# Feed-forward kernel whose second weight matrix is stored with reversed columns and streamed from the last column to the first

## The chip, the cores and the metric

The kernel runs on one core of one Trainium2 chip. The metric is device time in microseconds (us) for one execution of the whole program. A single execution was also taken by the hardware profiler; its rows are what the argument below is made from.

## The reference

The program computes three stages over 4608 tokens (8 batches of 576) of width 512. What matters here is the second, a dense feed-forward layer with a softplus between two products:

```
def _moe_ref(x, w_in, w_out):            # x 4608x512, w_in 512x2048, w_out 2048x512
    h = x @ w_in
    g = np.maximum(h, 0.0) + np.log1p(np.exp(-np.abs(h)))
    return (g @ w_out).astype(np.float32)

def reference(...):
    attn_out = _attn_ref(q, k, v)         # attention over keys pooled by 8; 8 heads of 64
    x = attn_out.transpose(0, 2, 1, 3).reshape(B * S, H * D)
    x = _moe_ref(x, w_in, w_out)          # the layer above
    return _moe2_ref(x, w_skip, w_gate, w1, w2)   # 8 experts, one per token, 512->1024->512, or skipped
```

## The kernel before, in words

The tokens are worked through in nine groups of 512 (`G`); `NG` is 9. For each group the attention of the next group runs in small pieces between the matmuls of the current one. The hidden width of 2048 is cut into 16 blocks `c` of 128.

`p1(g, c)` makes one block of the hidden layer: 12 matmuls accumulate `h`, 128 hidden rows by 512 tokens. ScalarE and VectorE then form the softplus and split it into a high part `gh` and a low part `gl`. `p2(g, c, gh, gl)` multiplies that block with rows `128c` to `128c+127` of the second matrix. It fills four PSUM tiles `y0` to `y3`, one for each 128 tokens of the group, and runs three matmuls into each: high by high, high by low, and low by high. In these matmuls the stationary operand (`lhsT`, loaded into the array ahead of the product) is a piece of `gh` or `gl`, 128 by 128. The moving operand (`rhs`, streamed through the array one column after the other) is the high or the low part of the second matrix, 128 by 512.

The loop calls `p1` for block `c` and, two blocks later, `p2` of that same block, so the softplus of a block has two blocks of time. `p2` is thus called 9 x 16 = 144 times with 12 matmuls each, 1728 matmuls in all (lines 641, 642 and 643, 576 each). The order on every engine is the order in which the program is written here.

The weights stay in SBUF for all nine groups. `_layout` packs them on the host with `words`: for each block `c`, 512 numbers of `w_in` and then 512 of `w_out`, in 8-byte form. `load_weights` fetches them once (tile `raw`), rebuilds 32-bit numbers from the two 4-byte halves, and writes their high and low parts into the tiles `wt`. There, in each row of 1024 numbers, columns 0 to 511 belong to `w_in` and columns 512 to 1023 to `w_out`. The two halves in `raw` are 4-byte numbers at a step of 8 bytes (`raw[:, :, 0]` and `raw[:, :, 1]`), so lines 455 and 458 read and write on ScalarE at that step and line 464 reads at it, while line 624 and line 628 work on plain consecutive 4-byte numbers.

After the last group the expert layer follows (`superblock`); its own matrices are `w1` and `w2`, and the lines of its products are 783 and 802 to 804.

Of the kernel before, what the change touches and what calls it, by code (L numbers as in the profile page):

```python
# [20 lines left out]
P = 128  # L21
# [13 lines left out]
def tile_kernel(ctx, tc, qT, kT, vT, wbits, w9, w1, w2, out):  # L35
# [364 lines left out]
    with ExitStack() as ph:  # L400
# [39 lines left out]
        def load_weights():  # L440


            bits = wbits.bitcast(I32)
            for c in range(16):
                if c % 2 == 0:
                    wt.append(wtile(f"wt{c // 2}", 2, 2, 1024, dtype=F32R))
                for j in range(2):
                    wh, wl = (wt[c // 2][:, c % 2, i, j * 512:(j + 1) * 512] for i in range(2))
                    raw = scratch.tile([P, 512, 2], I32, tag="raw", name="raw")
                    nc.sync.dma_start(out=raw.rearrange("p a b -> p (a b)"),  # L450
                                      in_=bits[c * P:(c + 1) * P, j * 1024:(j + 1) * 1024])
                    lo, hi = raw[:, :, 0], raw[:, :, 1]


                    nc.scalar.activation(out=hi.bitcast(F32), in_=hi.bitcast(F32), func=AF.Copy,
                                         scale=2.0 ** -112)

                    nc.scalar.activation(out=lo, in_=lo.bitcast(U32), func=AF.Copy, scale=7.49 * 2.0 ** -32)
                    yield
                    nc.vector.scalar_tensor_tensor(out=lo, in0=hi, scalar=3, in1=lo,  # L460
                                                   op0=ALU.logical_shift_left, op1=ALU.bitwise_or)
                    nc.vector.scalar_tensor_tensor(out=lo, in0=hi, scalar=-0x80000000, in1=lo,
                                                   op0=ALU.bitwise_and, op1=ALU.bitwise_or)
                    nc.scalar.activation(out=wh, in_=lo.bitcast(F32), func=AF.Copy)  # L464
                    yield
                    nc.vector.tensor_tensor(out=wl, in0=lo.bitcast(F32), in1=wh.bitcast(F32),
                                            op=ALU.subtract)
                    yield
# [164 lines left out]
        def p2(g, c, gh, gl):  # L633
            if c == 0:
                yps[g] = [ps_y.tile([P, D], F32, tag=f"y{t}", name=f"y{t}") for t in range(T)]
            w = wt[c // 2][:, c % 2]
            wh, wl = w[:, 0, 512:], w[:, 1, 512:]
            for t in range(T):
                th, tl = gh[:, t * P:(t + 1) * P], gl[:, t * P:(t + 1) * P]
                y = yps[g][t]  # L640
                nc.tensor.matmul(y, lhsT=th, rhs=wh, start=c == 0, stop=False)  # L641
                nc.tensor.matmul(y, lhsT=th, rhs=wl, start=False, stop=False)  # L642
                nc.tensor.matmul(y, lhsT=tl, rhs=wh, start=False, stop=c == 15)  # L643

        wl = load_weights()
# [45 lines left out]
        for g in range(NG):  # L691
            if g + 1 < NG:
                feed.start(units_of(g + 1), 6)
            for c in range(16):
                while loaded[0] < 6 * c + 3:
                    weights(1)
                pend.append((g, c, *p1(g, c)))
                weights(3)
                feed.tick()
                if len(pend) > 2:  # L700
                    item = pend.pop(0)
                    p2(*item)
                    if item[1] == 15:
                        ends.append(finish(item[0], yps[item[0]], lambda: ps_a, "pa"))
                if g == NG - 1:
                    last_group(c)
                weights(3)
                feed.tick()
                if loaded[0] == 96 and "cm9" not in ws:
                    scratch_cm.__exit__(None, None, None)  # L710
                    ws["cm9"] = ctx.enter_context(tc.tile_pool(name="cm9", bufs=1, side="right"))
                    ws["junk"] = ws["cm9"].tile([P, D], BF16, name="junk")
                    fill = ws["cm9"].tile([P, NCOL], I32, tag="fill", name="fill")
                    nc.gpsimd.memset(fill, int(BIG))
                    nc.sync.dma_start(out=tab.rearrange("(p c) b -> p (c b)", p=P), in_=fill)
            while g + 1 < NG and (feed.units or jobs or ends):
                feed.tick()
# [7 lines left out]
        hs = wtile("hs", 2, 8, SB, dtype=F32R)  # L725
        hh, hl = hs[:, 0], hs[:, 1]
        p2(*pend.pop(0))
        turn(0, ps_a, "pa")
        p2(*pend.pop(0))
        t = xp.tile([P, 4 * G], F32, tag="xl", name="xg1")  # L730
        xg[1] = [t[:, j * XW:(j + 1) * XW] for j in range(2)]
# [111 lines left out]
def _layout(q, k, v, moe_w_in, moe_w_out, moe2_w_skip, moe2_w_gate, moe2_w1, moe2_w2):  # L843
    import numpy as np
    B, H, S, Dh = q.shape

    def heads(a):
        return np.ascontiguousarray(a.reshape(B, H // 2, 2, S, Dh).transpose(0, 1, 2, 4, 3)).reshape(
            B * H // 2, 2 * Dh, S)

    def words(a, b):

        n = a.shape[1] // P
        return np.ascontiguousarray(np.concatenate([
            a.reshape(a.shape[0] // P, P, n, P).transpose(2, 1, 0, 3).reshape(n, P, -1),
            b.reshape(n, P, -1)], axis=2)).view(np.int64).reshape(n * P, -1)

    E, DM, F = moe2_w1.shape
    return {
        "qT": heads(q),  # L860
        "kT": heads(k),
        "vT": heads(v),
        "wbits": words(moe_w_in, moe_w_out),
        "w9": np.ascontiguousarray(np.concatenate([moe2_w_gate.T, moe2_w_skip[None, :]], axis=0)),
        "w1": np.ascontiguousarray(moe2_w1.reshape(E, DM // P, P, F).transpose(0, 2, 1, 3)).reshape(
            E * P, DM // P * F),
        "w2": np.ascontiguousarray(moe2_w2.reshape(E, F // P, P, DM).transpose(0, 2, 1, 3)).reshape(
            E * P, F // P * DM),
    }
# [18 lines left out]
```

## Time and profile before

| | |
|---|---|
| median of 3 runs | 1423.46 us (1421.79 to 1427.55) |
| the profiled execution's own time | 1429.72 us |
| its span, first to last instruction | 1428.0 us |
| TensorE matmuls (PE) busy | 1383.2 us, 97% of the span |
| TensorE weight loads (PEld) busy | 1151.9 us, 81% (beside the matmuls) |
| VectorE (DVE) busy | 844.4 us, 59% |
| ScalarE (ACT) busy | 643.2 us, 45% |
| GpSimd (POOL) busy | 313.7 us, 22% |
| mean granted TensorE clock | 0.994 of full speed |

Matmuls are pipelined: a matmul's busy time runs from its start until its result has left the array, and the next one starts before that. The pace of a stream of matmuls is therefore read from the distance between their starts, not from the busy time of one.

### The profile page before, as it was taken

The page shows a single profiled execution, that of the slowest core. Times are in us where ns is not written, and L with a number is a line of the kernel's source. Part 1 is how long each engine was busy: PE and PEld are TensorE (multiplying, and loading weights), DVE is VectorE, ACT ScalarE, POOL GpSimd, SP SyncE. Part 2 cuts the span into 40 slices and gives each one's busy share as a digit, 9 for nine tenths or more (in the row PEclk, how much of TensorE's full clock was granted, in tenths as well). Part 3 has the DMA queues.
Part 4 walks back from the last instruction along what each step waited for, and adds up shares of the span by engine and source line. Part 5 has one row for each costly group of instructions (what it writes and reads, how often), then busy time and mean ns, then how long its engine had stood idle before and what let it go on. Part 6 is the DMA issues. An engine that isn't in the chain of part 4 may idle for free. (4 is left out here: it accounts for less than half of the span.)

```text
span 1428.0 us, 21431 instructions
## 1 busy us (share of the span) xinstructions
PE 1383.2 (97%) x7434; PEld 1151.9 (81%) x7434; DVE 844.4 (59%) x2053; ACT 643.2 (45%) x1204; POOL 313.7 (22%) x365
## 2 busy tenths in 40 slices
PE   4999999999999999999999999999999999999996
PEld 3666877787878878778778778889998988999896
DVE  7888884784883973964954935654453422224254
ACT  5888655554554555555555455551111111113142
POOL 2010021021121121121030120143333433324232
PEclk9999999999999999999999999999999999999998
DMA  6545331131130230320310200502212111114051
GB/s 207 161 155 173 96 108 40 55 108 32 54 115 24 62 108 25 91 84 19 107 46 15 82 23 23 192 16 75 63 50 75 46 46 46 58 34 162 25 228 67
DMA packets 57691, 114.19 MB, mean 80 GB/s; under 512 B 17205, under 2 KB 23477, under 8 KB 56544
## 3 DMA queue, kind: packets, MB, share of 16 engines
q1 hardware_dynamic: 40032, 76.07, 17.3%
q0 software_dynamic: 17536, 36.60, 7.6%
q8 instruction: 62, 1.02, 0.3%
q14 instruction: 61, 0.50, 0.1%
HBM read 166.14 MB, written 29.67 MB: 137 GB/s over the span
## 5 line engine op out<-in xcount | busy, mean ns | idle before, releaser
L620 PE MATMUL h<-xh,wt 128*128 128x512 f32 x1152 | 389.3, 398 | 1.6 <-ACT wt L464 0.8
L620 PEld LDWEIGHTS h<-xh,wt 128*128 128x128 f32 x1152 | 217.1, 189 | 59.5 <-issue 10.4
L118 DVE CUSTOM_DVE_ANT_0 junk<-rows,w9b 128x512 bf16<-128x512 f32 x324 | 234.3, 723 | 9.3 <-ACT rows L112 3.7
L641 PE MATMUL y<-wt,gh 128*128 128x512 f32 x576 | 230.3, 400 | 2.1 <-ACT gh L628 2.1
L783 PE MATMUL h<-xt,w1h 128*128 128x256 f32 x1280 | 226.4, 281 | 3.2 <-ACT w1h L384 1.1
L620 PE MATMUL h<-xl,wt 128*128 128x512 f32 x576 | 226.3, 393 | 0.0
L643 PE MATMUL y<-wt,gl 128*128 128x512 f32 x576 | 224.6, 390 | 0.0
L642 PE MATMUL y<-wt,gh 128*128 128x512 f32 x576 | 224.6, 390 | 0.0
L783 PEld LDWEIGHTS h<-xt,w1h 128*128 128x128 f32 x1280 | 196.1, 188 | 6.0 <-issue 2.2
L626 DVE SCALAR_TENSOR_TENSOR a<-h,a 128x512 f32<-128x512 f32 x144 | 98.9, 687 | 169.6 <-ACT a L625 168.8
L787 ACT ACTIVATE hs<-h 128x512 fp32r<-128x512 f32 x80 | 47.4, 598 | 327.3 <-PE h L783 218.2
L623 ACT ACTIVATE a<-h 128x512 f32<-128x512 f32 x144 | 86.0, 598 | 226.3 <-PE h L620 195.8
L783 PE MATMUL h<-xt,w1l 128*128 128x256 f32 x640 | 179.4, 280 | 0.7 <-DVEq L833 0.7
L533 POOL TENSOR_TENSOR q<-q,st 64x144 f32<-64x144 f32 (+7 forms) x60 | 62.6, 1052 | 520.3 <-ACT xh L571 95.4
L628 ACT ACTIVATE gh<-a 128x512 fp32r<-128x512 f32 x144 | 90.8, 631 | 120.5 <-DVE a L626 119.3
L788 DVE SCALAR_TENSOR_TENSOR hs<-h,hs 128x512 fp32r<-128x512 f32 x80 | 54.7, 691 | 138.8 <-ACT hs L787 106.8
L641 PEld LDWEIGHTS y<-wt,gh 128*128 128x128 f32 x576 | 108.2, 188 | 28.2 <-ACT gh L628 2.9
L620 PEld LDWEIGHTS h<-xl,wt 128*128 128x128 f32 x576 | 108.7, 189 | 23.2 <-issue 2.8
L643 PEld LDWEIGHTS y<-wt,gl 128*128 128x128 f32 x576 | 108.1, 188 | 23.3 <-DVE gl L630 0.4
L642 PEld LDWEIGHTS y<-wt,gh 128*128 128x128 f32 x576 | 108.3, 188 | 20.4
L630 DVE TENSOR_TENSOR gl<-a,gh 128x512 fp32r<-128x512 f32 x144 | 99.3, 689 | 41.4 <-ACT gh L628 39.0
L783 PEld LDWEIGHTS h<-xt,w1l 128*128 128x128 f32 x640 | 122.2, 191 | 0.9 <-DVEq L833 0.9
(181 smaller groups left out, 1991.8 us busy)
## 6 DMA issues: line engine op xcount, KB each, us to landing
w9b<-w SPq DMA_DIRECT2D x81, 256.0 KB
raw<-wbits SPq DMA_DIRECT2D x32, 512.0 KB
x2d<-rows SPq DMA_DIRECT2D x36, 260.0 KB
kv<-kT SPq DMA_DIRECT2D x28, 288.0 KB
kv<-vT SPq DMA_DIRECT2D x28, 288.0 KB
q<-qT SPq DMA_DIRECT2D x8, 224.0 KB
q<-qT SPq DMA_DIRECT2D x8, 192.0 KB
q<-qT SPq DMA_DIRECT2D x8, 160.0 KB
```

The source lines that it names most:

```text
L118: nc.vector.tensor_tensor_reduce(out=ws["junk"], in0=rows[t][:, :D], in1=w9b[e], scale=1.0, scalar=0.0, op0=ALU.mult, op1=ALU.add, accum_o ...
L533: nc.gpsimd.tensor_tensor(out=ep_, in0=ep_, op=ALU.mult, in1=rc[:tp, h].unsqueeze(2).to_broadcast([tp, 2 * nt, SP]))
L620: nc.tensor.matmul(h, lhsT=l, rhs=r[:, kk, :], start=n == 0, stop=n == 11)
L623: nc.scalar.activation(out=a, in_=h, func=AF.Abs)
L626: nc.vector.scalar_tensor_tensor(out=a, in0=h, scalar=0.0, in1=a, op0=ALU.max, op1=ALU.add)
L628: nc.scalar.activation(out=gh, in_=a, func=AF.Copy)
L630: nc.vector.tensor_tensor(out=gl, in0=a, in1=gh.bitcast(F32), op=ALU.subtract)
L641: nc.tensor.matmul(y, lhsT=th, rhs=wh, start=c == 0, stop=False)
L642: nc.tensor.matmul(y, lhsT=th, rhs=wl, start=False, stop=False)
L643: nc.tensor.matmul(y, lhsT=tl, rhs=wh, start=False, stop=c == 15)
L783: nc.tensor.matmul(h[:, f2, :], lhsT=l, rhs=r[:, kk, :], start=n == 0, stop=n == 11)
L788: nc.vector.scalar_tensor_tensor(out=hl[:, fs, :], in0=h, scalar=0.0, in1=hh[:, fs, :].bitcast(F32), op0=ALU.max, op1=ALU.subtract)
```

## The change

The second matrix is stored on the host with its 512 columns in reverse order. The four-byte numbers of `wt[..., 512:1024]` so lie in the opposite order in SBUF, and `p2` reads them from column 1023 down to column 512, a step of minus one. Each product meets the same numbers in the same order as before, and the results land at the same places. Loads, splits and all other instructions are as they were.

```
--- before.py
+++ after.py
@@ -634,7 +634,7 @@
             if c == 0:
                 yps[g] = [ps_y.tile([P, D], F32, tag=f"y{t}", name=f"y{t}") for t in range(T)]
             w = wt[c // 2][:, c % 2]
-            wh, wl = w[:, 0, 512:], w[:, 1, 512:]
+            wh, wl = w[:, 0, 1023:511:-1], w[:, 1, 1023:511:-1]
             for t in range(T):
                 th, tl = gh[:, t * P:(t + 1) * P], gl[:, t * P:(t + 1) * P]
                 y = yps[g][t]
@@ -853,7 +853,7 @@
         n = a.shape[1] // P
         return np.ascontiguousarray(np.concatenate([
             a.reshape(a.shape[0] // P, P, n, P).transpose(2, 1, 0, 3).reshape(n, P, -1),
-            b.reshape(n, P, -1)], axis=2)).view(np.int64).reshape(n * P, -1)
+            b.reshape(n, P, -1)[:, :, ::-1]], axis=2)).view(np.int64).reshape(n * P, -1)
```

Row for row, the instructions of all five engines stand in the same order in both programs.

## Rows read from the trace of the kernel before

**Rows 1.** Page, head and busy times: us, share of the span, instructions.
```profile
span 1428.0 us, 21431 instructions
PE 1383.2 (97%) x7434; PEld 1151.9 (81%) x7434; DVE 844.4 (59%) x2053; ACT 643.2 (45%) x1204; POOL 313.7 (22%) x365
```

**Rows 2.** Windows, five stretches: length, busy and count by engine, granted clock, DMA.
```profile
core 0: us, PE busy (x) PEld busy (x) DVE busy (x) ACT busy (x) POOL busy (x), PEclk, DMA share, GB/s
33.00:60.00 27.00, 26.20 (x114) 17.66 (x113) 23.36 (x42) 22.52 (x47) 3.80 (x3) 0.91 0.40 126
60.00:120.00 60.00, 57.13 (x273) 42.57 (x273) 53.61 (x100) 53.21 (x106) 4.77 (x4) 0.97 0.54 170
120.00:960.00 840.00, 832.68 (x4002) 668.08 (x4000) 571.93 (x1532) 458.27 (x873) 137.57 (x160) 1.00 0.23 70
```

**Rows 3.** Waits of all engines, longest in total: us, times, longest one.
```profile
ACT a L623 <- PE h L620: 195.8, 106, 2.4
DVE a L626 <- ACT a L625: 168.8, 65, 4.9
```

**Rows 4.** Waits of the matmuls alone: us, times, longest one.
```profile
PE y L641 <- ACT gh L628: 2.1, 2, 1.2
```

**Rows 5.** Groups by line, TensorE: count, busy, mean ns, idle before and its releaser.
```profile
L641 PE MATMUL y<-wt,gh 128*128 128x512 f32 x576 | 230.3, 400 | 2.1 <-ACT gh L628 2.1
L643 PE MATMUL y<-wt,gl 128*128 128x512 f32 x576 | 224.6, 390 | 0.0
L642 PE MATMUL y<-wt,gh 128*128 128x512 f32 x576 | 224.6, 390 | 0.0
```

**Rows 6.** Matmuls in order of time, one call of `p2`: start us, us.
```profile
702.39 0.48 PE L641 MATMUL y<-wt,gh 128*128 128x512 f32 x1
702.71 0.40 PE L642 MATMUL y<-wt,gh 128*128 128x512 f32 x1
702.94 0.39 PE L643 MATMUL y<-wt,gl 128*128 128x512 f32 x1
703.17 0.39 PE L641 MATMUL y<-wt,gh 128*128 128x512 f32 x1
...
704.99 0.39 PE L643 MATMUL y<-wt,gl 128*128 128x512 f32 x1
```

**Rows 7.** Matmuls in order of time, expert layer, 256 columns: start us, us.
```profile
1040.00 0.28 PE L783 MATMUL h<-xt,w1l 128*128 128x256 f32 x1
1040.12 0.40 PE L783 MATMUL h<-xt,w1h 128*128 128x256 f32 x2
...
1042.12 0.28 PE L783 MATMUL h<-xt,w1l 128*128 128x256 f32 x1
```

**Rows 8.** The instructions that touch `wt`: ns min/median/max, first and last start us.
```profile
L641 PEld LDWEIGHTS y<-wt,gh x576: 186/188/190, 51.3 to 959.2; 128*128 128x128 f32 x192
L641 PE MATMUL y<-wt,gh x576: 387/389/504, 51.5 to 959.4; 128*128 128x512 f32 x192
L466 DVE TENSOR_TENSOR wt<-raw,wt x32: 674/692/1382, 13.7 to 147.2; 128x512 fp32r<-128x512 f32 x32
```

**Rows 9.** Groups by line and shape, ScalarE: count, busy, mean ns, idle before.
```profile
L624 ACT ACTIVATE a<-a 128x512 f32<-128x512 f32 x144 | 90.6, 629 | 3.0
L455 ACT ACTIVATE raw<-raw 128x512 f32<-128x512 f32 x32 | 21.4, 669 | 10.1 <-DMA raw<-wbits 10.0
L464 ACT ACTIVATE wt<-raw 128x512 fp32r<-128x512 f32 x32 | 21.3, 665 | 1.5 <-DVE raw L462 1.3
L628 ACT ACTIVATE gh<-a 128x512 fp32r<-128x512 f32 x144 | 90.8, 631 | 120.5 <-DVE a L626 119.3 <-issue 0.8
```

## What was predicted before the changed kernel ran

> **What bounds the kernel now.** I read the page first, then the stretches, then the waits, then the matmuls themselves in order of time. The page says that matmuls are in flight for 1383.2 of 1428.0 us [rows 1]. That share is an average, so I looked at where the changed products run: from 51.5 to 959.4 us [rows 8], nearly all of it in the stretch from 120 to 960 us. [...] The waits say the same from the other side: ScalarE waits 195.8 us in total for `h` from the first product, and VectorE 168.8 us for ScalarE [rows 3], while the matmuls that are changed wait 2.1 us in 2 waits over the whole run for their `gh` [rows 4]. So in this stage a nanosecond more or less on a `p2` matmul is a nanosecond on the kernel's time, with almost no cover. That settles how to price the change. It does not tell whether there is anything to price.
>
> **What one changed matmul takes.** Its busy time is 389 ns in the median [rows 8], and the three lines have 576 matmuls each [rows 5], but the pace is in the starts. In one call of `p2` the matmuls from the second to the twelfth start at 702.71 and 704.99 us, ten intervals in 2.28 us, so 228 ns each [rows 6]. 1728 such matmuls take 1728 x 0.228 = 394 us of TensorE's time, 28% of the span. A 256-column matmul of the same type shows how these 228 ns are made up: from 1040.00 to 1042.12 us there are six rounds of three (two high, one low), 18 intervals in 2.12 us, or 118 ns each [rows 7]. The difference, 110 ns for 256 columns, is 0.430 ns a column; and 228 - 512 x 0.430 leaves 8 ns that do not grow with the columns. So 220 of the 228 ns are the streaming of the moving operand, one column every 0.43 ns. This is the operand whose direction changes. The weight load beside it takes 188 ns [rows 8], less than the 228 ns, and its operand (`gh`, `gl`) keeps its direction.
>
> **The change part by part.** On the host the columns are stored the other way round: no device time. The load of the weights, the rebuilding on ScalarE and VectorE and the writes into `wt` (line 466 starts its last pass at 147.2 us [rows 8]) have the same instructions with the same sizes: 0. No instruction is added, removed or moved on any engine, and no wait is new, so nothing is queued behind anything else than before: 0. PSUM is written in the same order: 0.
>
> What is left is one term: 1728 moving reads with a step of minus one 4-byte number. No row of this trace has a read in descending order on any engine, so the term has to be bounded from both sides.
>
> [...]
>
> Above: the read of a row might get a small toll, or it might fall to a lower rate. For the small toll the nearest row is an engine that reads SBUF at another step than one. [...] For a lower rate, the stream that now takes one column in 0.43 ns would take two such steps: another 220 ns, say 228 with the rounding of whole matmuls, x 1728 = 394 us. If each column took four such steps, it would be three streams more, 1182 us.
>
> Which end is nearer? The row nearest in kind is ScalarE's: a changed step costs a pass there 35 to 40 ns, not a factor of two, though half the numbers it passes over are skipped. And in the reversed stream the next number always lies directly beside the last one, as before, and none is skipped. I take 0 for the term.
>
> The sum: 1428.0 + 0, for the profiled execution 1429.7 us. That execution was 6.3 us above the median of the runs, 1429.72 against 1423.46, so the time to expect for a median is **1423.5 us**.
>
> [...]
>
> **The rivals.**
> *Half rate in reverse.* The moving read serves two neighbouring numbers per step only when they ascend, and one otherwise. [...] Price: 394 us, less what TensorE's idle time could swallow. In the stretches where `p2` runs it is 27 - 26.20, 60 - 57.13 and 840 - 832.68, together 11 us [rows 2]; other engines would have more room than now. So 383 to 394 us more, 1423.5 + 389 = about 1812 us. This is the case that ends on the other side, and it decides as soon as a changed matmul starts more than 4 ns later than now (0.5% of 1423.5 is 7.1 us, over 1728). [...] With four steps in place of one it is about 2605 us.
> *A toll for each matmul.* The address counter or the first fetch at the far end costs a few ns. Between the 8 ns of fixed time once more, 14 us, and the 6% of ScalarE's row, 24 us: 1437 to 1447 us. For it speaks that a fixed part exists; against it, that the start of a read is already overlapped with the last matmul's stream, as the even starts show [rows 6].
> *A gain.* The fixed 8 ns vanish: 1423.5 - 14 = about 1410 us. Nothing in the rows speaks for it.
> *The change does not do what it says.* If the read were turned into an ascending one on the way to the chip, the result would carry the second matrix mirrored, and the time would be that of no change. This can't be told from my forecast by time, and is counted in with it.
>
> **How the numbers follow.** About 0.5% is what a measurement of this kernel can tell from no change; the three runs of before lie 0.4% apart. No change: 0.81. Half rate or lower: 0.11 (half or the page's rate 0.10, a quarter 0.01). A toll of 14 to 24 us: 0.06. A gain: 0.02. The forecast is the first, 1423.5 us; its own range is 1418 to 1430 by the spread of the runs, which holds it in some 95 of 100 cases, 0.77. To reach 8 in 10, I extend the upper end into the toll, to 1440 us, which takes about half of its 0.06; the half rate is left out, since nothing lies between. Faster by over 0.5%: the gain and 0.01 of chance in the first case, 0.03. Slower: 0.11 + 0.06 and 0.01 of chance, 0.18. Within 0.5%: 0.79.
>
> **What would show it.** In the profile of the changed kernel the starts of lines 641 to 643 within a call of `p2` are 228 ns apart and their median busy time is 389 ns; lines 620 keep theirs; the stretch from 120 to 960 us is as long as before, and TensorE is as full. A toll would show as starts at 236 to 242 ns in `p2` alone. Half rate would show as starts near 450 ns, `p2` near 5.4 us a call, and the expert layer beginning some 390 us later, with ScalarE and VectorE less busy in share. What would make the prediction wrong is that one number: the distance of two starts in lines 641 to 643. If it stays and the time still moves by more than 0.5%, my reading that only this operand's stream is touched is wrong.

## The result and the profile after

The changed kernel takes 1435.19 us in the median of 3 runs (1433.87 to 1435.46) against 1423.46 us before, 11.7 us between the medians; the ratio on record is 1.0062 with a 95% interval of 1.0039 to 1.0085, or 5.6 to 12.1 us. It is slower by a little, and the likeliest case of the prediction, no change at all, did not come true. Five more rounds (the run e4_again below) gave 1.0068, from 1.0054 to 1.0082, which is 9.7 us, from 7.7 to 11.7 us. A small toll, which the prediction held as a rival, is what happened, smaller than the 14 to 24 us at which it was priced there.

The head of the page of the changed kernel, to be held against [rows 1]:

```profile
span 1433.7 us, 21431 instructions
PE 1394.8 (97%) x7434; PEld 1152.6 (80%) x7434; DVE 843.9 (59%) x2053; ACT 643.5 (45%) x1204; POOL 311.5 (22%) x365
```

The count of instructions is the same, and only TensorE's busy time has moved by more than 3 us, by 11.6 us. The two spans lie just 5.7 us apart, because the profiled execution of before took 1429.72 us where the median of its runs was 1423.46 us. The stretch of [rows 2] in which most of `p2` runs, and the waits that answer to [rows 3] and [rows 4]:

```profile
120.00:960.00 840.00, 836.72 (x3966) 662.50 (x3965) 566.78 (x1528) 455.04 (x868) 135.17 (x160) 1.00 0.23 70
```

```profile
ACT a L623 <- PE h L620: 213.5, 110, 2.4
DVE a L626 <- ACT a L625: 173.0, 66, 5.0
PE y L641 <- ACT gh L628: 0.4, 1, 0.4
```

In the same 840 us TensorE is busy a little longer (836.72 against 832.68 us) and starts 36 matmuls fewer (3966 against 4002), at the same granted clock of 1.00. ScalarE waits longer for it (213.5 against 195.8 us). So TensorE itself became slower, and the waits of `p2` did not grow. The groups of the changed lines, against [rows 5], and two of the instructions that touch `wt`, against [rows 8]:

```profile
L641 PE MATMUL y<-wt,gh 128*128 128x512 f32 x576 | 234.6, 407 | 0.6 <-ACT gh L628 0.4
L642 PE MATMUL y<-wt,gh 128*128 128x512 f32 x576 | 229.4, 398 | 0.0
L643 PE MATMUL y<-wt,gl 128*128 128x512 f32 x576 | 228.8, 397 | 0.0
```

```profile
L641 PEld LDWEIGHTS y<-wt,gh x576: 186/188/190, 52.5 to 968.1; 128*128 128x128 f32 x192
L641 PE MATMUL y<-wt,gh x576: 394/397/506, 52.7 to 968.4; 128*128 128x512 f32 x192
```

The median of a changed matmul went from 389 to 397 ns, while the weight load beside it still takes 188 ns. Now the starts, for one call of `p2` and for the end of another with the `p1` behind it, against [rows 6]:

```profile
705.10 0.40 PE L643 MATMUL y<-wt,gl 128*128 128x512 f32 x1
705.33 0.40 PE L620 MATMUL h<-xh,wt 128*128 128x512 f32 x1
705.57 0.39 PE L620 MATMUL h<-xl,wt 128*128 128x512 f32 x1
...
708.41 0.40 PE L642 MATMUL y<-wt,gh 128*128 128x512 f32 x1
708.65 0.40 PE L643 MATMUL y<-wt,gl 128*128 128x512 f32 x1
...
710.75 0.40 PE L643 MATMUL y<-wt,gl 128*128 128x512 f32 x1
```

From the second to the twelfth start there are ten intervals in 2.34 us, so 234 ns each where it was 228. Taken over all calls, the median distance of two starts in lines 641 to 643 is 233 ns, before 227 ns. (From here on "spacing" means the median distance of two starts, worked out from the starts in the trace; the rows round to 10 ns.) Six nanoseconds times 1728 matmuls are 10.4 us.

### The profile page after: what moved, and what is told of

The parts are those of the page before. It is cut to its first block, busy times and chain, and to the rows that moved or that the text cites. A ratio compares the mean times of both kernels' runs of the same rounds, so it can differ in the third digit from the quotient of the medians.

```text
span 1433.7 us, 21431 instructions
## 1 busy us (share of the span) xinstructions
PE 1394.8 (97%) x7434; PEld 1152.6 (80%) x7434; DVE 843.9 (59%) x2053; ACT 643.5 (45%) x1204; POOL 311.5 (22%) x365
## 5 line engine op out<-in xcount | busy, mean ns | idle before, releaser
L620 PEld LDWEIGHTS h<-xh,wt 128*128 128x128 f32 x1152 | 217.0, 189 | 61.7 <-issue 10.4
L641 PE MATMUL y<-wt,gh 128*128 128x512 f32 x576 | 234.6, 407 | 0.6 <-ACT gh L628 0.4
L642 PE MATMUL y<-wt,gh 128*128 128x512 f32 x576 | 229.4, 398 | 0.0
L643 PE MATMUL y<-wt,gl 128*128 128x512 f32 x576 | 228.8, 397 | 0.0
L623 ACT ACTIVATE a<-h 128x512 f32<-128x512 f32 x144 | 85.9, 596 | 238.1 <-PE h L620 213.5
```

The source lines that it names most:

```text
L620: nc.tensor.matmul(h, lhsT=l, rhs=r[:, kk, :], start=n == 0, stop=n == 11)
L623: nc.scalar.activation(out=a, in_=h, func=AF.Abs)
```

## The experiments

The theory after the result was: the descending read makes each of these matmuls some 6 ns longer, and nothing else plays a part. The rivals were that the storage or the data do it, and that the place or the start of the read does. Within the theory it was open whether the toll is paid once for a matmul, for each column, or for something else.

**e1_store_only.** The storage without the read. The lines show the edit against the changed kernel; the gating matrix is mirrored too, so that every token goes to the same expert as before.

```
-            wh, wl = w[:, 0, 1023:511:-1], w[:, 1, 1023:511:-1]
+            wh, wl = w[:, 0, 512:], w[:, 1, 512:]
```

> Second matrix stored with reversed columns, but read in ascending order; the rows of the gating matrix are mirrored too, so that every token goes to the same expert as before, and the output's dense part is left mirrored. If the descending read costs the time: starts of lines 641 to 643 go back from 234 to 228 ns, median busy from 397 to 389 ns, ratio to before 1.000 +- 0.003. If the layout in memory or the data cost it (rival): 234 ns and a ratio near 1.006 stay.

Measured: ratio 0.9987 (0.9973 to 1.0001), spacing 227 ns, and the matmuls as they were before the change:

```profile
L642 PE MATMUL y<-wt,gh x576: 387/389/489, 48.5 to 955.9; 128*128 128x512 f32 x192
```

The storage costs nothing that these runs can tell; the difference hangs on the direction of the read.

**e2_both_products.** The change, and the same direction in the first product.

```
-                    nc.tensor.matmul(h, lhsT=l, rhs=r[:, kk, :], start=n == 0, stop=n == 11)
+                    nc.tensor.matmul(h, lhsT=l, rhs=r[:, kk, ::-1], start=n == 0, stop=n == 11)
```

> The change, and also the moving operand of the first product (line 620, 512 tokens) read from the last column to the first; the tokens of a group are left in reversed order. If any 512-column descending read pays the toll: line 620 goes from 389 to 397 ns busy and from 228 to 234 ns between starts, 1728 more matmuls x 6 ns = some 10 us on top of the change, ratio to before near 1.014. If the toll belongs to the second product (its tile is shared with the weight loads of the first, or its place in the row), line 620 stays at 389 ns and the ratio at about 1.006 to 1.008.

Measured: ratio 1.0108 (1.0092 to 1.0123), median 1441.22 us. The instructions of line 620 and of line 641:

```profile
L620 PE MATMUL h<-xh,wt x1152: 394/398/796, 33.8 to 966.0; 128*128 128x512 f32 x192
```

```profile
L641 PE MATMUL y<-wt,gh x576: 395/398/504, 54.0 to 974.9; 128*128 128x512 f32 x192
```

The first product pays the toll as the second does, on another tile: 398 in place of 389 ns, spacing 233 in place of 227 ns. The total rose by 0.0040 on top of the change, 5.7 us, where 10 us were expected. The starts say why. After a call of `p2` with descending reads, the first two intervals of an ascending `p1` are 238 and 232 ns, in the rows above 705.33 to 705.57 and on; before the change they are 227 ns both. With both products descending that extra is gone. And where a piece of the attention stands ahead of a `p1`, its ascending intervals are 229 to 233 ns for half the call anyway, so that 233 ns is little more. From the first to the last start of line 641 the changed kernel takes 915.7 us (52.7 to 968.4) and e2 920.9 us (54.0 to 974.9), so 5.2 us more; that agrees with the totals.

**e3_expert_256.** The kernel of before, with descending reads in the expert layer's first product.

```
-                            nc.tensor.matmul(h[:, f2, :], lhsT=l, rhs=r[:, kk, :],
+                            nc.tensor.matmul(h[:, f2, :], lhsT=l, rhs=r[:, kk, ::-1],
```

> Kernel of before with one edit: the first product of the expert layer (line 783, 1920 matmuls with 256 columns in this trace) reads its moving operand from the last column to the first; the tokens of a block are left in reversed order. Toll once for each matmul, whatever its length: starts from 118 to 124 ns, busy from 281 to 289 ns, 1920 x 6 = 11.5 us in the expert stage. Toll for each column (6 ns / 512 = 0.012 ns): starts to 121 ns, busy to 285 ns, 5.8 us.

Measured: ratio 1.0006 (0.9994 to 1.0018). Both expectations failed:

```profile
L783 PE MATMUL h<-xt,w1h x1280: 279/282/389, 957.7 to 1400.5; 128*128 128x256 f32 x183
```

The median is 282 ns where it was 281, and the mean distance of two starts within the line (those under 150 ns) is 117.8 ns where it was 117.0. A descending read of 256 columns is all but free.

**e4_again.** The changed kernel, five rounds.

> The changed kernel once more, in five rounds. By the starts (6 ns x 1728 = 10.4 us, all on the path): ratio to before 1.0073. By the drift seen in the profiled pair between the first and the last changed matmul (7.8 us): 1.0055. If the first measurement was chance: 1.000.

Measured: 1.0068 (1.0054 to 1.0082); six runs of 1428.79 to 1436.33 us against 21 runs of before from 1422.74 to 1430.15 us. Both estimates lie in the interval, so the total does not choose between them.

```profile
L641 PE MATMUL y<-wt,gh x576: 394/397/504, 47.9 to 961.6; 128*128 128x512 f32 x192
```

The runs e5 to e11 below change the second product's result, and with it the routing of tokens, so their totals are not compared; the spacing is read from one execution each.

**e5_mix_order.** Each 128-token tile of `p2` reads in its own order; `V` is `w[:, i, 512:]` cut into 128 blocks of four.

```
 t == 0:  w[:, i][:, 512:]              # ascending, lines 642 to 644
 t == 1:  w[:, i][:, 1023:511:-1]       # descending, lines 647 to 649
 t == 2:  V[:, ::-1, :]                 # blocks descending, inside ascending, 652 to 654
 t == 3:  V[:, :, ::-1]                 # blocks ascending, inside descending, 657 to 659
```

> One look, starts within each call of the second product; the four 128-token tiles read the second matrix in four ways: ascending; descending; blocks of four numbers in descending order with the four ascending; blocks of four in ascending order with the four descending. The columns of three tiles so come out permuted, which also changes where tokens are routed, so only the spacing in the second product is read. Toll once per matmul for a start at the far end: ascending 228, descending 234 ns, and the block forms 228 to 234 by where they start. Toll for the order within four neighbours: first block form 228, second 234. Toll for the order of the blocks of four: first block form 234, second 228.

One call in order of time:

```profile
456.74 0.39 PE L643 MATMUL y<-wt,gh 128*128 128x512 f32 x1
456.96 0.39 PE L644 MATMUL y<-wt,gl 128*128 128x512 f32 x1
...
457.43 0.40 PE L648 MATMUL y<-wt,gh 128*128 128x512 f32 x1
457.66 0.40 PE L649 MATMUL y<-wt,gl 128*128 128x512 f32 x1
...
458.13 0.40 PE L653 MATMUL y<-wt,gh 128*128 128x512 f32 x1
458.36 0.40 PE L654 MATMUL y<-wt,gl 128*128 128x512 f32 x1
...
458.83 0.40 PE L658 MATMUL y<-wt,gh 128*128 128x512 f32 x1
459.07 0.39 PE L659 MATMUL y<-wt,gl 128*128 128x512 f32 x1
```

Over some 143 calls the three spacings of each tile (the last one to the next tile) are 227, 227, 227; 234, 238, 231; 233, 233, 233; and 240, 232, 231 ns. Both block forms pay on average what the plain descending read pays. So neither the order within four neighbours nor that of the blocks of four is alone to blame. Whether the first block form pays for its steps back or for its short inner runs of four is not separated here.

**e6_mix_start.** The same reading by tile, with other starts, another length and another step.

```
 t == 0:  w[:, i][:, 511:1023]      # lines 646 to 648
 t == 1:  w[:, i][:, 1020:508:-1]   # lines 651 to 653
 t == 2:  w[:, i][:, 1023:767:-1]   # 256 columns, lines 656 to 658
 t == 3:  w[:, i][:, 1023::-2]      # lines 661 to 663
```

> One look, the same reading by tile; block 0 of each group stays ascending. Tile 0 reads ascending from column 511 (one number before a group of four begins), tile 1 descending from 1020 (the first of a group of four) to 509, tile 2 only 256 columns, descending, tile 3 every second number descending from 1023 (so half of these come from the first matrix). The second product's result is changed in all four. If the alignment of the start makes the toll: tile 0 at 234 and tile 1 at 228 ns. If the direction makes it: tile 0 at 228 and tile 1 at 234. Tile 2: 124 ns with a toll per matmul, 121 with a toll per column. [...]

```profile
470.72 0.39 PE L647 MATMUL y<-wt,gh 128*128 128x512 f32 x1
470.94 0.39 PE L648 MATMUL y<-wt,gl 128*128 128x512 f32 x1
...
471.40 0.40 PE L652 MATMUL y<-wt,gh 128*128 128x512 f32 x1
471.64 0.40 PE L653 MATMUL y<-wt,gl 128*128 128x512 f32 x1
...
472.67 0.65 PE L662 MATMUL y<-wt,gh 128*128 128x512 f32 x1
473.14 0.65 PE L663 MATMUL y<-wt,gl 128*128 128x512 f32 x1
```

Spacing between the second and the third matmul of each tile: 228 ns ascending from an odd place, 236 ns descending from 1020, 118 ns for 256 descending, 467 ns for every second number descending. The start's place has no part in the toll; the direction has.

**e7_mix_size.** Lengths, and the ascending control for the step of two.

```
 t == 0:  w[:, i][:, 512:768]       # 256 ascending, lines 646 to 648
 t == 1:  w[:, i][:, 1023:639:-1]   # 384 descending, lines 651 to 653
 t == 2:  w[:, i][:, 512:896]       # 384 ascending, lines 656 to 658
 t == 3:  w[:, i][:, 0:1024:2]      # lines 661 to 663
```

> One look, the same reading by tile; block 0 of each group stays whole and ascending. Tile 0: 256 columns ascending; tile 1: 384 descending; tile 2: 384 ascending; tile 3: 512 numbers ascending at every second place (half of them from the first matrix). The second product's result is changed in all four. Controls: 118 ns for 256, 173 ns for 384 ascending (8 + 0.430 x 384). 384 descending: 179 with a toll per matmul, 177.5 with a toll per column. [...]

Measured in the same way: 118 ns for 256 ascending, 182 ns for 384 descending, 174 ns for 384 ascending, and for every second number ascending 453 ns:

```profile
451.72 0.63 PE L662 MATMUL y<-wt,gh 128*128 128x512 f32 x1
452.18 0.63 PE L663 MATMUL y<-wt,gl 128*128 128x512 f32 x1
```

Spaced by 453 ns ascending and 467 ns descending (e6), a read at a step of 8 bytes takes twice the 227 ns of neighbouring numbers, in either direction. With tiles of different forms beside each other the values for 384 are uneven (180, 182, 176 against 179, 174, 174), so a run with one form per group followed (e11_sizes).

**e8_half_weights and e9_half_weights_sizes.** Is a toll on short reads hidden under the weight load? All tiles use half of the stationary columns.

```
 lhsT=th[:, :64] (and tl), output y[:64, :n]
 e8: 512 ascending, 512 descending, 256 ascending, 256 descending
 e9: 384 ascending, 384 descending, 128 ascending, 128 descending
```

> One look, starts within each call of the second product, read by 128-token tile; blocks 0 and 15 of each group stay whole and ascending. All four tiles use only 64 of the 128 columns of the stationary operand, so that the weight load is about half as long. Tile 0: 512 ascending, tile 1: 512 descending, tile 2: 256 ascending, tile 3: 256 descending. The second product's result is changed in all four. So far 256 columns showed 118 ns in both directions. If that is because the weight load is what 256 columns wait for, and a toll of 6 ns per matmul lies hidden under it: tile 2 falls below 118 ns (to 107 to 115) and tile 3 lies 6 ns above tile 2; tiles 0 and 1 are 227 and 233. If a read of 256 columns pays no toll: tiles 2 and 3 equal. If the toll comes from the weight load running beside the descending read: tile 1 falls to 227 to 230.

> As the run with half weights, other lengths. Tile 0: 384 ascending, tile 1: 384 descending, tile 2: 128 ascending, tile 3: 128 descending. Toll per matmul: tile 1 lies 6 ns above tile 0, tile 3 lies 6 ns above tile 2 unless the weight load hides it. Toll per column: 4.5 ns and 1.5 ns.

The descending tile of 512 columns in e8, its weight loads and its products:

```profile
L652 PEld LDWEIGHTS y<-wt,gh x126: 134/137/228, 54.0 to 885.3; 128*64 128x64 f32 x126
L652 PE MATMUL y<-wt,gh x126: 394/397/632, 54.2 to 885.5; 128*64 128x512 f32 x126
```

The weight load took 133 to 138 in place of 188 ns in the median, by line, which is 0.71 to 0.73 of it and not the half that was expected. Spacing between second and third matmul: 229 and 233 ns for 512, 117 and 120 ns for 256, 173 and 178 ns for 384, 59 and 60 ns for 128 columns, ascending and descending. A tile's three intervals are uneven, so their sums belong beside them: 356 ascending and 353 descending for 256 columns, 523 and 525 for 384, 690 and 701 for 512 (the ascending tile of the last two stands first behind `p1`, and its first interval is the longest of its three). 256 ascending did not fall with the shorter load, so the load is not what short reads wait for, and no 6 ns lay hidden there. The descending read of 512 pays with a short load too. In e9 the granted clock was 0.95 from 200 to 700 us, so its means are not used, only medians.

**e10_two_level.** Steps back, but far apart; `B(n)` is `w[:, i, 512:]` cut into blocks of `n`.

```
 t == 0:  B(4)                  # the same as plain ascending, lines 646 to 648
 t == 1:  B(256)[:, ::-1, :]    # halves swapped, lines 651 to 653
 t == 2:  B(64)[:, ::-1, :]     # lines 656 to 658
 t == 3:  B(256)[:, :, ::-1]    # halves ascending, inside descending, lines 661 to 663
```

> One look, full weights, starts within each call read by tile; blocks 0 and 15 of each group stay whole and ascending. Tile 0: 512 ascending as a control. Tile 1: the two halves of 256 swapped, each ascending (one step back in the whole read). Tile 2: eight pieces of 64 in descending order, each ascending. Tile 3: two halves in ascending order, each of 256 descending. The columns of the second product's result are permuted. If the toll is that of any read that is not one ascending run: 233 ns in tiles 1, 2 and 3. If it is paid for each step against the direction of memory: tile 1 227, tile 2 227 to 228, tile 3 233. If only a descending read of more than 256 pays: tile 3 at 227.

```profile
458.83 0.39 PE L652 MATMUL y<-wt,gh 128*128 128x512 f32 x1
459.05 0.39 PE L653 MATMUL y<-wt,gl 128*128 128x512 f32 x1
...
459.51 0.39 PE L657 MATMUL y<-wt,gh 128*128 128x512 f32 x1
459.73 0.39 PE L658 MATMUL y<-wt,gl 128*128 128x512 f32 x1
...
460.19 0.40 PE L662 MATMUL y<-wt,gh 128*128 128x512 f32 x1
460.43 0.40 PE L663 MATMUL y<-wt,gl 128*128 128x512 f32 x1
```

Spacing 227 ns in all three intervals of the first three tiles; 232, 240 and 231 ns in the fourth. A read that goes back in blocks of 64 is free here (227 ns); two descending runs of 256 in one matmul pay, though a matmul of 256 descending columns by itself does not (118 ns in e6, as ascending in e7).

**e11_sizes.** One length and direction for each group of 512 tokens, 14 calls of 12 matmuls each.

```
 g == 1: w[:, i, 512:896]    g == 2: w[:, i, 895:511:-1]   # 384, lines 647 and 651
 g == 3: w[:, i, 512:960]    g == 4: w[:, i, 959:511:-1]   # 448, lines 655 and 659
 g == 5: w[:, i, 512:832]    g == 6: w[:, i, 831:511:-1]   # 320, lines 663 and 667
 g == 7: w[:, i, 512:768]    g == 8: w[:, i, 767:511:-1]   # 256, lines 671 and 675
```

> One look. Blocks 1 to 14 of the second product read, in groups 1 to 8 of 512 tokens in turn, 384 ascending, 384 descending, 448 ascending, 448 descending, 320 ascending, 320 descending, 256 ascending, 256 descending, so that each form runs 14 calls of 12 matmuls alone; the rest of the columns is left out, so the result is changed. Read: starts within a call. Ascending by 8 + 0.430 n: 173, 201, 146, 118 ns. Toll per matmul: each descending form 6 ns above. Toll per column (0.012 ns): 4.5, 5.3, 3.8, 3.0 ns above. Descending read as a limit of rate, 233 ns / 512 = 0.455 ns a column, which only binds where it is longer than the ascending spacing: 175 (+2), 204 (+3), 146 (0), 118 (0).

Mean spacing from the third to the last matmul of a call that follows directly on `p1`, ascending and descending: 256 columns 120.0 and 118.8 ns, 320 columns 146.7 and 146.4 ns, 384 columns 175.9 and 177.8 ns, 448 columns 202.2 and 206.9 ns. The busy times move with the length too, in a row for each:

```profile
L647 PE MATMUL y<-wt,gh x112: 333/334/432, 172.2 to 250.3; 128*128 128x384 f32 x112
```

```profile
L651 PE MATMUL y<-wt,gh x112: 337/342/434, 265.8 to 345.9; 128*128 128x384 f32 x112
```

The toll on the spacing in these means is thus nothing for 256 and 320 columns, and 2, 5 and (from the changed kernel) 6 ns for 384, 448 and 512. The 2 ns at 384 are a mean over uneven calls: after their first intervals (up to 185 ns) the ascending ones settle at 173 to 174 ns, and against that the descending 178 ns are 4 to 5 more. So the toll is absent up to 320 columns and there from 384 on. Neither "once per matmul" nor "per column" fits over all lengths. The estimate of a limit of 0.455 ns a column (233 ns / 512) fits up to 320; at 384 it asks for 175 where 178 was measured, at 448 for 204 where 207 was.

**e12_blocks64.** The change with blocks of 64 columns in place of single columns, in storage and in the read.

```
-            wh, wl = w[:, 0, 512:], w[:, 1, 512:]
+            wh, wl = (w[:, i, 512:].rearrange("p (a b) -> p a b", b=64)[:, ::-1, :] for i in range(2))
-            b.reshape(n, P, -1)], axis=2)
+            b.reshape(n, P, 8, 64)[:, :, ::-1].reshape(n, P, -1)], axis=2)
```

> The second matrix stored with its eight blocks of 64 columns in reverse order and read block by block backwards, each block ascending; all else as before. If only steps back inside the stream at the scale of single numbers cost: starts at 227 ns, busy 389 ns, ratio 1.000 +- 0.002. If any read that is not one ascending run costs: 233 ns, ratio 1.007.

Measured: 0.9987 (0.9971 to 1.0004), spacing 227 ns.

```profile
L642 PE MATMUL y<-wt,gh x576: 387/389/492, 54.2 to 960.5; 128*128 128x512 f32 x192
```

## Why the prediction was partly right

*The stage and its bound* were read rightly: most of the change lies in `p2`, TensorE is the only full engine there (busy for 836.72 of 840 us, VectorE for 566.78), and no instruction was added or moved. The 8 ns and 0.430 ns a column held too: for 320 and 448 columns they ask for 146 and 201 ns, and 147 and 202 ns were measured (e11). e1_store_only shows that host layout, loads and splits cost nothing, as priced. One sign was not as forecast: line 620 was to keep its starts, and its first two intervals after a `p2` went from 227 to 238 and 232 ns.

*The step that failed* is "I take 0 for the term". It rested on the thought that a stream in which the next number always lies beside the last one must run as fast backwards as forwards. It does not: 1728 reads take 6 ns more each (227 ns in e1, 233 in the changed kernel and in e4). Both ends that had been set up around it were off. The toll of the rival, 14 to 24 us, was mis-sized: its lower end took the 8 ns of fixed time once more and its upper end the 6% of ScalarE's passes in [rows 9] (665 and 669 against 629 and 631 ns), which no run shows on TensorE at a step of minus one; 6 ns, 2.6%, were measured there. The toll is not a second fixed part either, since up to 320 columns pay next to nothing (117.8 against 117.0 ns for 256 in e3, 146.4 against 146.7 for 320 in e11). Half rate or lower did not come at a step of minus one. Of the 0.10 for such rates, the one that stands beside the half is shown by no run; in place of either, 512 descending columns took 233 ns where 227 were before.

*The range* holds the measured 1435.19 us, but the reasoning does not lead there. The case that it was built on had 1418 to 1430 us and the toll 1437 to 1447, and the time fell between the two; it is inside because the upper end was extended to 1440 to reach 8 in 10. A time within 0.5% had 0.79, and the five rounds show it slower by 0.54 to 0.82%. That the range held is in good part luck.

*The row chosen as nearest* misled in both directions. ScalarE loses 6% when it reads numbers 8 bytes apart (by 34 to 40 of some 630 ns, [rows 9]); TensorE's stream takes twice as long at that step (453 against 227 ns, e7). A row of another engine could not stand in for TensorE's stream. The half rate exists, then, but for a step of two (453 ns, e7; 467 ns descending, e6) and not for a step of minus one (233 ns).

*Almost no cover* was right for about three quarters. Six nanoseconds on 1728 matmuls are 10.4 us. From the first to the last start of line 641 the time rose from 907.9 us ([rows 8], 51.5 to 959.4) to 915.7 us (52.7 to 968.4), 7.7 us before rounding. Since both traces have the same matmuls in the same order, the growth can be summed interval by interval. Inside the calls of `p2` it is 9.6 us, and at the step to a following `p1` and inside it 2.1 us. Against that, the steps from either product to a piece of the attention became 2.3 us shorter, and four long intervals in the first 150 us together 1.8 us; what is left is under 0.2 us. Other traces put the same stretch at 907.4 (e1), 907.0 (e3) and 906.2 us (e12) ascending and 913.7 us (e4) descending, so the pairs differ by 5.8 to 9.5 us. The totals' 9.7 us (7.7 to 11.7) lie at the upper end; whether more than the stretch contributes is not shown.

*What stays open* is why the descending read costs more at all, and why it does so only from somewhere between 320 and 384 columns on; the mechanisms that the rivals suppose are shown by no run. What is shown is that the start's place (e6), the length of the weight load (e8), the tile (e2) and far steps back (e10, e12) are not the cause. A collision with one of the other engines is unlikely too. From 120 us on, the intervals of `p2` beside which ScalarE alone worked, VectorE alone, both, or either or both with GpSimd all have medians of 227 ns before and 233 ns after (11 to 277 intervals each, from the fourth start of a call on).

## What to carry to other kernels

Where a stage is bound by TensorE's streaming, price an edit of the moving operand's access pattern from a run with that very pattern on TensorE; rows of another engine don't stand in for it. Keep the innermost step of a long moving operand at plus one: at 512 columns reversed blocks of 64 are free (227 ns, e10 and e12), reversed blocks of four or single numbers cost some 3% (233 ns, e5), and a step of two doubles the time (453 ns, e7). All of this is for 4-byte numbers; no run here reverses 2-byte ones. And read a change of a few nanoseconds from the starts of thousands of matmuls, where it shows at once, before the total, whose runs lie 0.5% apart.

## What the runs showed that had not been expected

- A descending moving operand of 4-byte numbers adds no more than 1 ns at 256 and 320 columns, 2 to 5 ns at 384, 5 ns at 448 and 6 ns at 512 to the spacing of matmuls (e3, e11, the changed kernel).
- Switching direction costs too: the first two ascending matmuls after a descending stream are spaced 238 and 232 ns apart, then 227 ns (69 calls of the changed kernel); with both products descending it is 233 ns throughout (e2).
- A step of 8 bytes in the moving operand takes 453 ns ascending and 467 ns descending for 512 numbers, against 227 ns for neighbouring ones (e6, e7).
- Blocks of four in reverse order cost as much as a descending read (233 ns, e5), steps back every 64 or 256 numbers nothing (227 ns, e10).
